# Fewer closing waits on SyncE, and denominators one group later, in a two-branch attention kernel

## The chip, the cores and the metric

One core of one Trainium2 chip. The metric is the device time of one execution in microseconds (us), lower is better. The profile's span is shorter than that time: it runs from the first to the last instruction of the kernel. In the first profiled execution the span was 493.6 us and the time 495.56 us.

All runs of this case were in the fast state, and the mean of TensorE's granted clock over an execution was 0.996 to 1.000 of full speed in all of them.

## The reference, cut to what matters

```python
g = sigmoid((x * gate_w).sum(-1))            # x: 2048 x 1024, bf16
a = A(x)                                     # linear attention, 32 heads of 32
b = B(x)                                     # local attention, 8 keys, every second one
return g * a + (1 - g) * b

# in A: phi(t) = where(t > 0, t + 1, exp(t)) + 1e-6
kv  = einsum("bhsd,bhse->bhde", phi(k), v)
z   = einsum("bhsd->bhd", phi(k))
num = einsum("bhqd,bhde->bhqe", phi(q), kv)
den = einsum("bhqd,bhd->bhq", phi(q), z)[..., None] + 1e-6
o   = num / den                              # then @ wo
```

## The kernel before

The program is written as a list of operations with what they read and write; a small scheduler in Python puts them into an order for each engine, and `emit` adds semaphores. Each DMA channel has a semaphore of its own; there are 81. The scheduler's guess of a DMA's latency decides only the order:

```python
            o.end = t + o.cost
            free[e] = o.end
            fin = o.end
            if o.chan is not None:
                dma_free = max(dma_free, o.end) + o.lat
                fin = dma_free + 2.0          # when users of this DMA may be placed
```

In branch A, queries are taken in four chunks `u` of 512 positions, eight column groups `j` each. When a chunk's eight groups of phi(q) are there, `over(u)` makes the denominators of all heads in one small set of matmuls, inverts them as exp(-ln), sends them to memory and loads them back spread over the partitions, and DVE multiplies phi(q) by them:

```python
        def over(u):
            ...
            P.op("pe", fn, 0.55, mode="c", reads=[zsel.all(), tgt.part((0, 8), (c0, c0 + 512))], ..., name="den")
            R, rs = RAr.next()
            P.op("act", ... ACT.Ln ...); P.op("act", ... ACT.Exp, scale=-1.0 ...)
            for c in range(4):                # store: rc_hbm <- ra
                P.op("sp", ...)
            for j in range(8):                # load: rb <- rc_hbm, then multiply
                B, bs = RBr.next()
                ...
                last_in[0] = P.op("sp", lambda e, B=B, src=src: e.dma_start(B[:, :], src), 0.5, ..., chan="rci%d" % bs, lat=1.0)
                P.op("dve", lambda e, B=B, dst=dst: e.tensor_tensor(dst, dst, B[:, :], ALU.mult), 0.65, reads=[reg, B.all()], writes=[reg])
        ...
        for n, (u, j) in enumerate(nums):
            numer(u, j)
            if j == 7:
                after(3, lambda u=u: over(u))
            slot(0)
```

The formulas used for speed hold only for inputs in a certain range, so the kernel computes a flag, and every engine tests it at its end. If it is 0, a general version (`general_path`) runs and overwrites the output. With this data the flag is 1, so every engine takes a branch over its copy of the general version:

```python
    def tail(e, eng):
        reg = e.alloc_register("fast_ok")
        e.wait_ge(*flag_op.val)
        e.reg_load(reg, flag[0:1, 0:1])
        if eng == "sp":
            for s, v in P.final:              # all 81 DMA channels
                e.wait_ge(s, v)
        with e.If_eq(reg, 0):
            for s, v in P.final + [(P.esem[x], n) for x, n in P.counts.items() if n]:
                e.wait_ge(s, v)
            for th in progs[eng]:             # the general version
                th(e)
```

Of the kernel before, what the change touches and what calls it, by code (L numbers as in the profile page):

```python
# [24 lines left out]
class Tile:  # L25
# [13 lines left out]
    def all(self):  # L39
        return [(self.space, self.lo, self.lo + self.row * self.size, self)]  # L40
# [15 lines left out]


class Op:
    __slots__ = ("eng", "fn", "cost", "deps", "prio", "seq", "chan", "lat", "pos", "val", "users", "raw", "name", "mode", "start", "end")


class Prog:
# [13 lines left out]
        self.held = {}  # L76
        self.read = set()

    def op(self, eng, fn, cost, reads=(), writes=(), prio=None, chan=None, lat=0.0, after=(), name="", mode="m"):
        o = Op()  # L80
        o.eng, o.fn, o.cost, o.prio, o.chan, o.lat, o.name, o.mode = eng, fn, cost, prio, chan, lat, name, mode
        if prio is None:
            o.prio = 1000 + len(self.ops)
        o.seq = len(self.ops)
        o.deps = set(after)
        o.raw = set(after)
        o.users = []
        rd = [iv for r in reads for iv in r]
        wr = [iv for w in writes for iv in w]
        for sp, lo, hi, own in rd:  # L90
            for rec in self.recs.get(sp, ()):
                if rec[0] < hi and lo < rec[1]:
                    if rec[3]:
                        o.deps.add(rec[2])
                        o.raw.add(rec[2])
                    elif sp == "P" and (rec[2].eng != eng or eng == "any"):
                        o.deps.add(rec[2])
        for sp, lo, hi, own in wr:
            for rec in self.recs.get(sp, ()):
                if rec[0] < hi and lo < rec[1]:  # L100
                    o.deps.add(rec[2])
                    if sp != "P" and rec[4] is not own:
                        o.raw.add(rec[2])
        o.deps.discard(o)
        o.raw.discard(o)
        for sp, lo, hi, own in wr:
            lst = self.recs.setdefault(sp, [])
            lst[:] = [r for r in lst if not (lo <= r[0] and r[1] <= hi)]
            lst.append((lo, hi, o, True, own))
        for sp, lo, hi, own in rd:  # L110
            self.recs.setdefault(sp, []).append((lo, hi, o, False, own))
        for sp, lo, hi, own in rd + wr:
            if sp == "P" and own is not None:
                self.held.setdefault(own, []).append(o)
                if eng != "pe":
                    self.read.add(own)
        self.ops.append(o)
        return o

    def schedule(self, dma_rate=0.2e6):  # L120
        for o in self.ops:
            for d in o.deps:
                d.users.append(o)
        left = {o: len(o.deps) for o in self.ops}
        ready_at = {o: 0.0 for o in self.ops}
        free = {e: 0.0 for e in self.ENGS}
        dma_free = 0.0
        wait = {e: [] for e in self.ENGS}
        avail = {e: [] for e in self.ENGS}

        def ready(o, at):
            if o.eng == "any":

                est = []
                for e in ("act", "dve"):
                    q = sum(x[2].cost for x in avail[e] if x[0] < o.prio) + sum(x[2].cost for x in wait[e] if x[2].prio < o.prio and x[0] < at + 0.3)
                    est.append((max(free[e], at) + q + o.cost[e], e))
                o.eng = min(est)[1]
                o.fn, o.cost = o.fn[o.eng], o.cost[o.eng]
            heapq.heappush(wait[o.eng], (at, o.seq, o))  # L140

        for o in self.ops:
            if left[o] == 0:
                ready(o, 0.0)
        self.order = {e: [] for e in self.ENGS}
        mode = "m"
        done = 0
        while done < len(self.ops):
            best = None
            for e in self.ENGS:  # L150
                while wait[e] and wait[e][0][0] <= free[e]:
                    _, _, o = heapq.heappop(wait[e])
                    heapq.heappush(avail[e], (o.prio, o.seq, o))
                if avail[e]:
                    t = free[e]
                elif wait[e]:
                    t = wait[e][0][0]
                else:
                    continue
                if best is None or t < best[0]:  # L160
                    best = (t, e)
            assert best is not None, "no operation can go"
            t, e = best
            if not avail[e]:
                while wait[e] and wait[e][0][0] <= t:
                    _, _, o = heapq.heappop(wait[e])
                    heapq.heappush(avail[e], (o.prio, o.seq, o))
            _, _, o = heapq.heappop(avail[e])
            if e == "pe":

                if o.mode != mode and mode != "m":
                    near = [x for x in avail[e] if x[2].mode == mode and x[0] < o.prio + 30]
                    if near:
                        x = min(near)
                        avail[e].remove(x)
                        heapq.heapify(avail[e])
                        heapq.heappush(avail[e], (o.prio, o.seq, o))
                        o = x[2]
                if o.mode != mode:
                    t += 0.09  # L180
                mode = o.mode
            o.start = t
            o.end = t + o.cost
            free[e] = o.end
            fin = o.end
            if o.chan is not None:
                dma_free = max(dma_free, o.end) + o.lat
                fin = dma_free + 2.0
            o.pos = len(self.order[e])
            self.order[e].append(o)  # L190
            done += 1
            for u in o.users:
                lat = self.LAT[o.eng] if (u.eng != o.eng or o in u.raw) and o.chan is None else 0.0
                if u.eng == o.eng == "pe":
                    lat = 0.0
                ready_at[u] = max(ready_at[u], fin + lat)
                left[u] -= 1
                if left[u] == 0:
                    ready(u, ready_at[u])
        self.span = max(free.values())  # L200

    def emit(self, block, tail):
        for e in self.ENGS:
            self.esem[e] = self.sem("e_" + e)
        chan_n = {}
# [5 lines left out]
        for o in order:  # L211
# [10 lines left out]
            deps = sorted(o.deps, key=lambda d: -d.start)  # L222
            for d in deps:
# [3 lines left out]
                s, v = d.val  # L227
# [16 lines left out]
            tail(e, eng)  # L244

        self.final = [(self.csem[c], n) for c, n in chan_n.items()]
        self.counts = cnt
        block.sync(lambda e: run(e, "sp"))
        block.scalar(lambda e: run(e, "act"))
# [853 lines left out]
def build_kernel(nc, A_x, A_wqkv, A_wo, B_x, B_wqkv, B_wo, gate_w, out):  # L1103
# [117 lines left out]
    def plan(seen):  # L1221
# [241 lines left out]
        def after(n, f, cols=False):  # L1463
            later.append((slot_n[0] + n, f, cols))
            later.sort(key=lambda x: x[0])
# [112 lines left out]
        def over(u):  # L1578
# [16 lines left out]
            for j in range(8):  # L1595
                B, bs = RBr.next()
                src = rc_hbm[u, 4 * j:4 * j + 4, :, :].rearrange("r k n -> (r k) n")[:, None, :].to_broadcast([16, 8, 512])
                last_in[0] = P.op("sp", lambda e, B=B, src=src: e.dma_start(B[:, :], src), 0.5, reads=[[("R", 4 * u + j // 2, 4 * u + j // 2 + 1, None)]], writes=[B.all()],  # L1598
                                  chan="rci%d" % bs, lat=1.0)
                dst, reg = tgt[:, j, c0:c0 + 512], tgt.part((j, j + 1), (c0, c0 + 512))  # L1600
                P.op("dve", lambda e, B=B, dst=dst: e.tensor_tensor(dst, dst, B[:, :], ALU.mult), 0.65, reads=[reg, B.all()], writes=[reg])  # L1601

# [46 lines left out]
        for n, (u, j) in enumerate(nums):  # L1649
            numer(u, j)  # L1650
            if j == 7:
                after(3, lambda u=u: over(u))
            slot(0)
            if n in (2, 4, 6, 8):
                fold((n - 2) // 4, (n - 2) // 2 % 2)
            if n >= 20:
                a_out(*outs.pop(0))
                slot(0)
# [48 lines left out]
    def tail(e, eng):  # L1707
        reg = e.alloc_register("fast_ok")
        e.wait_ge(*flag_op.val)
        e.reg_load(reg, flag[0:1, 0:1])  # L1710
        if eng == "sp":
            for s, v in P.final:
                e.wait_ge(s, v)
        with e.If_eq(reg, 0):
            for s, v in P.final + [(P.esem[x], n) for x, n in P.counts.items() if n]:
                e.wait_ge(s, v)
            for th in progs[eng]:
                th(e)
# [37 lines left out]
```

## Time and profile before

| | |
|---|---|
| time, median of the first 3 runs | 495.04 us (494.76 to 495.15) |
| span of the profiled execution | 493.6 us |
| TensorE busy | 97% of the span, granted clock 0.998 |
| longest TensorE wait after 320 us | 0.98 us, third denominator |
| last store issued / landed | 488.97 / 491.05 us |
| SyncE's 81 waits | 490.00 to 492.82 us |

The page of the kernel before: the span; the busy time, share and instruction count of each engine; and the chain that ended last.

```profile
span 493.6 us, 11394 instructions
PE 477.7 (97%) x5055; PEld 226.2 (46%) x5121; DVE 274.7 (56%) x487; ACT 166.9 (34%) x287; POOL 5.1 (1%) x27
...
PE 89%; DMA 3%; SPq 3%; issue 2%; DVE 2%; ACT 1%; ACTq 0%
```

TensorE bounds this kernel. (5055 matmuls against 5121 weight loads: 66 matmul records are missing from this trace, so the busy time is a little too low.) What is to be won lies in TensorE's few waits, in the head before it starts, and in the tail after it ends. The table of TensorE's waits from 320 to 494 us names one wait worth a look: engine, line, what it waited for, total us, times, longest us.

```profile
PE ps_all L1585 <- DVE xT L1326: 1.0, 1, 1.0
PE ps_all L1313 <- issue: 0.3, 2, 0.2
```

The timeline around it (start, duration, engine, line, operation, count, and in brackets the idle time ahead with what ended it) shows how it comes about. L1601 is the multiplication by the reciprocals, L1326 the last step of phi, L1585 the denominator matmul.

```profile
362.04 0.69 DVE L1601 TENSOR_TENSOR xT<-xT,rb 128x512 bf16<-128x512 bf16 x1 [1.38 <-DMA rb<-rc_hbm]
...
369.60 0.69 DVE L1601 TENSOR_TENSOR xT<-xT,rb 128x512 bf16<-128x512 bf16 x1 [1.00 <-DMA rb<-rc_hbm]
370.21 0.68 DVE L1326 SCALAR_TENSOR_TENSOR xT<-ps_all,e 128x512 bf16<-128x512 f32 x1
370.95 0.62 PE L1585 MATMUL ps_all<-xT,zsel 128*32 128x512 bf16 x8 [0.98 <-DVE xT L1326]
```

DVE stands 1.38 and 1.00 us at multiplications whose reciprocals have not landed; the phi behind them in its queue starts only at 370.21 us, behind the multiplication of 369.60 us, and TensorE waits 0.98 us for it.

The tail is not on the page, since waits and branches are not counted as busy. It stands in the trace's records of single instructions, printed here (start in us, duration in ns, operation, semaphores that it waits for):

```
Sync   488.971  432 DMA_DIRECT2D      last store
Sync   489.459  503 TENSOR_LOAD       the flag
Sync   490.004   28 EVENT_SEMAPHORE   173, 172
...    38 more with two waits each, about 61 ns apart
Sync   492.790   28 EVENT_SEMAPHORE   212, 133
Sync   492.857   58 COMPARE_BRANCH    132
Sync   493.362   57 DRAIN
Vector 488.655   72 COMPARE_BRANCH
Vector 491.538   58 DRAIN
```

### The profile page before, as it was taken

Reading aid. Unit: us, or ns where it says so; the run is one execution under the profiler, and the core shown is the slowest. Engines: PE = TensorE matmul, PEld = TensorE weight load, DVE = VectorE, ACT = ScalarE, POOL = GpSimd, SP = SyncE. Lnnn points to the kernel's source line nnn. Section 1 sums busy time; section 2 is a strip of 40 time slices with the busy share of each in tenths; the row PEclk is TensorE's granted clock in tenths of the full one; section 3 lists DMA queues with packets and bytes.
Section 4 is the critical chain, followed back from the end, with each engine's and each line's share of the span. In section 5 each row is a group of like instructions: output and inputs, shape, how many; then the busy total and the mean of one; then the engine's idle time right before and its main releaser. Section 6 shows DMA issues by size and latency. Waiting matters only on the chain.

```text
span 493.6 us, 11394 instructions
## 1 busy us (share of the span) xinstructions
PE 477.7 (97%) x5055; PEld 226.2 (46%) x5121; DVE 274.7 (56%) x487; ACT 166.9 (34%) x287; POOL 5.1 (1%) x27
## 2 busy tenths in 40 slices
PE   8999999999999999999999999999999999999995
PEld 3444444444444445545554544444444444444442
DVE  2112345899676785564555555596865735524443
ACT  2111111222334345656565465455432223020000
POOL 3000000000000000000000000000000000000000
PEclk9999999999999999999999999999999999999999
DMA  8989992222003155111010100503564325101122
GB/s 225 212 206 322 307 371 62 86 86 85 14 23 110 29 161 141 28 36 35 24 35 25 35 3 3 171 1 80 124 182 117 76 38 153 65 1 66 65 85 68
DMA packets 51067, 48.80 MB, mean 99 GB/s; under 512 B 20161, under 2 KB 38977, under 8 KB 51010
## 3 DMA queue, kind: packets, MB, share of 16 engines
q1 hardware_dynamic: 50466, 47.47, 34.5%
q8 instruction: 42, 0.69, 0.6%
q10 hardware_dynamic: 544, 0.52, 0.3%
q14 instruction: 15, 0.12, 0.1%
HBM read 34.34 MB, written 9.44 MB: 89 GB/s over the span
## 4 chain that ended last, share of the span: by engine, by line
PE 89%; DMA 3%; SPq 3%; issue 2%; DVE 2%; ACT 1%; ACTq 0%
PE ps_all L1313 71%; PE ps_all L1634 11%; PE ps_all L1405 2%; PE ps_all L1424 2%; DMA rb<-rc_hbm 1%; SPq L1287 1%; PE ps_all L1506 1%; SPq L1598 1%; DMA w<-in_B_wqkv_dram 1%; PE ps_all L1431 1%; DMA rc_hbm<-ra 1%; DVE zsel L1548 1%; SPq L1292 1%; DVE pq L1326 0%; PE ps_all L1585 0%
## 5 line engine op out<-in xcount | busy, mean ns | idle before, releaser
L1313 PE MATMUL ps_all<-w,xT 128*128 128x512 bf16 x921 | 207.5, 380 | 5.4 <-issue 4.3
L1313 PE MATMUL ps_all<-xT,w 128*128 128x512 bf16 x748 | 167.5, 379 | 2.3 <-issue 1.7
L1313 PEld LDWEIGHTS ps_all<-w,xT 128*128 128x128 bf16 x960 | 91.3, 98 | 109.8 <-DMA xT<-in_A_x_dram 1.8
L1313 PEld LDWEIGHTS ps_all<-xT,w 128*128 128x128 bf16 x768 | 73.7, 98 | 89.1 <-issue 1.8
L1634 PE MATMUL ps_all<-w,qT 128*128 128x512 bf16 (+1 forms) x259 | 55.3, 373 | 0.3
L1634 PEld LDWEIGHTS ps_all<-w,qT 128*128 128x128 bf16 x264 | 25.8, 98 | 29.7
L1324 DVE TENSOR_SCALAR e<-e 128x512 bf16<-128x512 bf16 x64 | 18.3, 291 | 33.8 <-ACT e L1320 17.2
L1344 DVE CAST vst<-ps_all 128x512 bf16<-128x512 f32 x15 | 10.4, 692 | 44.0 <-PE ps_all L1313 44.0
L1411 ACT ACTIVATE E<-ps_all 128x1824 bf16<-128x1824 f32 (+1 forms) x18 | 30.4, 1687 | 9.8 <-PE ps_all L1405 9.0
L1322 ACT ACTIVATE e<-ps_all 128x512 bf16<-128x512 f32 x32 | 19.1, 597 | 42.8 <-PE ps_all L1313 42.8
L1414 DVE TENSOR_TENSOR E<-E,msk 128x1824 bf16<-128x1824 bf16 (+1 forms) x18 | 19.8, 1102 | 22.1 <-ACT E L1411 22.1
L1638 DVE SCALAR_TENSOR_TENSOR o<-ps_all,gm,xT 128x512 bf16<-128x512 f32 (+1 forms) x25 | 18.2, 730 | 23.0 <-PE ps_all L1634 22.8
L1320 ACT ACTIVATE e<-ps_all 128x512 bf16<-128x512 f32 x32 | 19.1, 597 | 26.8 <-PE ps_all L1313 25.8
L1345 ACT ACTIVATE vst<-ps_all 128x512 bf16<-128x512 f32 x17 | 10.1, 597 | 47.7 <-PE ps_all L1313 47.7
L1274 DVE TENSOR_TENSOR mx<-mx,kT 128x1024 bf16<-128x1024 bf16 x32 | 20.8, 688 | 9.3 <-ACT kT L1345 9.2
L1274 DVE TENSOR_TENSOR mx<-mx,qT 128x1024 bf16<-128x1024 bf16 x32 | 20.8, 687 | 6.9 <-ACT qT L1348 6.7
L1443 DVE TENSOR_TENSOR qT<-ps_all,L 128x456 bf16<-128x456 f32 (+1 forms) x36 | 21.0, 627 | 6.2 <-ACT L L1441 5.0
L1326 DVE SCALAR_TENSOR_TENSOR pk<-ps_all,e 128x512 bf16<-128x512 f32 x32 | 21.9, 688 | 0.7
L1440 ACT ACTIVATE L<-ps_all 128x456 f32<-128x456 f32 (+1 forms) x36 | 17.8, 547 | 12.4 <-PE ps_all L1424 12.4
L1345 ACT ACTIVATE kT<-ps_all 128x512 bf16<-128x512 f32 x16 | 9.6, 597 | 35.8 <-PE ps_all L1313 35.8
L1601 DVE TENSOR_TENSOR xT<-xT,rb 128x512 bf16<-128x512 bf16 x24 | 16.3, 689 | 8.7 <-DMA rb<-rc_hbm 8.5
L1348 ACT ACTIVATE qT<-ps_all 128x512 bf16<-128x512 f32 x16 | 9.6, 597 | 31.5 <-PE ps_all L1313 31.5
(72 smaller groups left out, 284.1 us busy)
## 6 DMA issues: line engine op xcount, KB each, us to landing
rb<-rc_hbm SPq DMA_DIRECT2D x32, 256.0 KB, 5.1
w<-in_A_wqkv_dram SPq DMA_DIRECT2D x6, 1024.0 KB, 8.5
v<-vB_hbm SPq DMA_DIRECT2D x36, 128.0 KB, 2.9
vB_hbm<-vst SPq DMA_DIRECT2D x32, 128.0 KB, 5.9
w<-in_B_wqkv_dram SPq DMA_DIRECT2D x4, 1024.0 KB, 9.0
xn<-in_A_x_dram SPq DMA_DIRECT2D x16, 256.0 KB, 2.7
out_dram<-o SPq DMA_DIRECT2D x15, 256.0 KB, 2.0
w<-in_A_wo_dram SPq DMA_DIRECT2D x8, 256.0 KB, 4.1
```

What stands on the lines that cost most here:

```text
L1274: P.op("dve", lambda e, m=m, op=op: e.tensor_tensor(m[:, 0:n], m[:, 0:n], src, op), 0.08 + n / 1920.0, reads=[m.all(), reg], writes=[m.all()],
L1313: last = e.matmul(bank.ap(), lhs(dc), rhs(dc), start=(dc == 0), stop=(dc == 7))
L1320: P.op("act", lambda e: e.activation(e_[:, :], bank.ap(), ACT.Exp), act(512), reads=[bank.iv], writes=[e_.all()])
L1322: P.op("act", lambda e: e.activation(e_[:, :], bank.ap(), ACT.Exp, accum_out=qe[:, col:col + 1]), act(512) + 0.1, reads=[bank.iv], writes= ...
L1324: P.op("dve", lambda e: e.tensor_scalar(e_[:, :], e_[:, :], 1.0, 1e-6, op0=ALU.min, op1=ALU.add), 0.25, reads=[e_.all()], writes=[e_.all()])
L1326: P.op("dve", lambda e: e.scalar_tensor_tensor(out=dst, in0=bank.ap(), scalar=0.0, in1=e_[:, :], op0=ALU.max, op1=ALU.add), dps(512), read ...
L1345: fa = lambda e: e.activation(dst, src(), ACT.Copy)
L1411: P.op("act", lambda e: e.activation(E[:, 0:32 * nq].rearrange("p (j q) -> p j q", j=4), ps[:, 4:8, 0:8 * nq], ACT.Exp), act(32 * nq), rea ...
L1414: P.op("dve", lambda e: e.tensor_tensor(ev(), ev(), m[:, :, :].rearrange("p r q -> p (r q)")[:, None, :].to_broadcast([128, 16, 2 * nq]), ...
L1443: P.op("dve", lambda e, L=L, h=h, q0=q0: e.tensor_tensor(qT[:, :, q0:q0 + nq], SO[h].ap(0, n).rearrange("p (c q) -> p c q", c=8), L[:, 0:n ...
L1634: last = e.matmul(bank.ap(0, f1 - f0), qT[:, dc, t * 128:(t + 1) * 128], ws[3][:, dc, f0:f1], start=(dc == 0), stop=(dc == 7))
L1638: P.op("dve", lambda e, bank=bank, o_=o_, t=t, n=n, i0=i0, i1=i1, tgt=tgt, c0=c0: e.scalar_tensor_tensor(out=o_[:, i0 * 128:i1 * 128].rear ...
```

## The change

The intent: SyncE should not go through 81 waits when nearly all of those DMAs have been waited for by somebody who used their data; only the 4 channels of output stores have no other waiter. And the wait on the reciprocals should go away: each chunk's denominators one slot later, and 2.5 us more latency assumed for the loads, so that the scheduler puts the multiplications further back in DVE's queue. The diff, cut to its core:

```diff
-                fin = dma_free + 2.0
+                fin = dma_free + o.pad          # pad=2.0 unless given
...
+    def awaited(self, chan):
+        return all(o.users for o in self.ops if o.chan == chan)
...
         self.final = [(self.csem[c], n) for c, n in chan_n.items()]
+        self.last = [(self.csem[c], n) for c, n in chan_n.items() if not self.awaited(c)]
...
-                                  chan="rci%d" % bs, lat=1.0)
+                                  chan="rci%d" % bs, lat=1.0, pad=4.5)
...
-                after(3, lambda u=u: over(u))
+                after(4, lambda u=u: over(u))
...
         if eng == "sp":
-            for s, v in P.final:
+            for s, v in P.last:
                 e.wait_ge(s, v)
```

More of the change, by code (lines that the diff above doesn't have):

```diff
@@ L58 @@
 class Op:
-    __slots__ = ("eng", "fn", "cost", "deps", "prio", "seq", "chan", "lat", "pos", "val", "users", "raw", "name", "mode", "start", "end")
+    __slots__ = ("eng", "fn", "cost", "deps", "prio", "seq", "chan", "lat", "pos", "val", "users", "raw", "name", "mode", "pad", "start", "end")
 class Prog:
@@ L77, in __init__, with op @@
         self.read = set()
-    def op(self, eng, fn, cost, reads=(), writes=(), prio=None, chan=None, lat=0.0, after=(), name="", mode="m"):
+    def op(self, eng, fn, cost, reads=(), writes=(), prio=None, chan=None, lat=0.0, after=(), name="", mode="m", pad=2.0):
         o = Op()
+        o.pad = pad
         o.eng, o.fn, o.cost, o.prio, o.chan, o.lat, o.name, o.mode = eng, fn, cost, prio, chan, lat, name, mode
```

## The prediction

> **What bounds it.** TensorE. The page gives PE 477.7 of 493.6 us busy (97%), clock 0.998; the chain of waits is 89% PE. From 320 us on, the table of waits has one PE stall of note: the third denominator matmul waits 0.98 us (at 370.95 us) for DVE's phi (L1326), because DVE, in order, stood 1.38 and 1.00 us waiting for reciprocal loads (rb, 362.04 and 369.60 us). The tail: the last matmul ends at 488.0 us, DVE at 488.55, the span at 493.64.
>
> **The tail before, from the instruction records.** SyncE issues the last store at 488.97 us, reads the flag, and goes through 81 waits, two to an instruction: 490.00 to 492.82 us, about 61 ns each. The last store had landed at 491.05 us, so 1.8 us of this is overhead. Then branch 492.86, drain 493.36, and 0.28 us of closing barrier.
>
> **What changes.** Instruction order is identical up to about 334 us.
> 1. The denominators come one to three groups later, and the multiplications that wait for rb stand later in DVE's queue. PE does the same work, so the most to be had is the 0.98 us stall. Normalised chunks stay in time: chunk 0 was multiplied out by 353.1 us, and the first output group that reads it moves later too. I expect -1.0 us.
> 2. 36 SyncE instructions disappear, so SyncE reaches its branch right after the last landing: 1.8 us earlier. But the branch jumps over 145 fallback instructions. [...]branch to drain took 2.88 us on DVE, 2.45 on ACT, 2.54 on POOL, each with an 8 KiB instruction packet about 1 us after the branch[...]. On SyncE it took only 0.50 us. SyncE's own fetches, at 97.0 and 491.6 us, and a 0.4 us hiccup at 490.55 put a block boundary just after its 207th instruction[...]. After the change the branch is about the 203rd instruction, before that boundary[...]. So I estimate that the branch now misses: 2.45 to 2.9 us in place of 0.50, giving back 2.0 to 2.4 us for the 1.8 us saved. Net tail: about +0.4 us. If the fetch was started anyway, the tail gains 1.7 us.
>
> **Sum.** Miss (70%): 495.04 - 1.0 + 0.4 = about 494.4 us. Hit (30%): 495.04 - 1.0 - 1.7 = about 492.3 us. Median 494.2 us; 8 in 10: 492.0 to 495.0. Faster by over 2%: 0.01; within 2%: 0.98; slower: 0.01.
>
> **What would show it.** (a) The wait of the denominator matmul on DVE's phi goes from 0.98 us to about 0, and the last matmul ends about 1 us earlier. (b) SyncE has 2 wait instructions before the branch, and the branch starts within 0.15 us of the last landing. (c) Branch to drain on SyncE grows to about 2.5 us, with a new 8 KiB instruction fetch after the branch; if (c) is absent, the hit case.
>
> **What would make it wrong.** A straggling last landing (one of 16 came 0.38 us after the others); a new PE wait on a normalised chunk; the fetch being ahead of where I place it.

(In this text instructions are counted from 0: the branch is number 239 before and 203 after, its target 385 and 349. Two of the expectations below count the same ones from 1.)

What the trace of before shows: branch to drain took 2.88 us on DVE, 2.45 on ACT and 2.54 on POOL, each with an 8 KiB instruction packet 0.92 to 1.05 us after the branch (489.70, 444.57 and 433.45 us); on SyncE it took 0.50 us, and packets start at 491.58 and 492.36 us, 1.27 and 0.50 us ahead of that branch, the next one at 493.92 us, after the drain. Which of them are SyncE's the author read from their times. That a fetch makes the difference, and that a boundary lies behind number 207, is the estimate from these times and the 0.40 us hiccup; the expectations below call it the fetch theory, and group 2 tests where the branch turns slow.

## The result, and the profile after

495.53 us median (495.31 to 496.11, 6 runs) against 495.1 us (494.76 to 496.3, 6 runs): ratio 1.0008, 95% interval 0.9995 to 1.002. Ratios here are the mean time of one kernel's fast runs over that of the other's of the same rounds, so not quite the ratio of the medians. The forecast was 494.2 us, 492.0 to 495.0: the class (within 2%) was right, the range was missed by 0.5 us.

The table of TensorE's waits after, same stretch, has only its headings: the wait is gone.

```profile
core 0 of [0], span 494.1 us
engine line waited for: us in total, times, longest us
```

The timeline after at the same place (lines of the file have moved by 6: L1607, L1332 and L1591 answer to L1601, L1326 and L1585):

```profile
370.76 0.69 DVE L1607 TENSOR_TENSOR xT<-xT,rb 128x512 bf16<-128x512 bf16 x1 [0.33 <-DMA rb<-rc_hbm]
...
372.12 0.69 DVE L1332 SCALAR_TENSOR_TENSOR xT<-ps_all,e 128x512 bf16<-128x512 f32 x1
372.69 0.61 PE L1591 MATMUL ps_all<-xT,zsel 128*32 128x512 bf16 x8
```

SyncE's tail, by single instructions as above:

```
Sync   489.024  433 DMA_DIRECT2D      last store (landed 491.250)
Sync   489.514  517 TENSOR_LOAD       the flag
Sync   491.084   17 EVENT_SEMAPHORE   211
Sync   491.267   28 EVENT_SEMAPHORE   212, 209
Sync   491.337   58 COMPARE_BRANCH    208
Sync   493.857   63 DRAIN             2.52 us after the branch (before: 0.50)
```

Both parts of the forecast are there: no wait, and a branch that reaches its place 0.09 us after the last landing and then takes 2.52 us. From the end of the last DVE operation to the span's end it is 5.57 us now, 5.09 before. Yet TensorE's last matmul started at 487.77 us, as before (487.76): the microsecond of the wait did not come out. It had been lost at the other end. The timelines of both at the first score matmul (a matmul of branch B), of before:

```profile
5.62 14.69 PE L1313 MATMUL ps_all<-w,xT 128*128 128x512 bf16 x62 [0.35 <-DMA xT<-in_A_x_dram]
...
125.78 0.70 PE L1405 MATMUL ps_all<-qT,kT 32*64 32x57 bf16 x64
```

and of after:

```profile
5.97 14.37 PE L1319 MATMUL ps_all<-w,xT 128*128 128x512 bf16 x58 [0.70 <-DMA xT<-in_A_x_dram]
...
126.89 0.70 PE L1411 MATMUL ps_all<-qT,kT 32*64 32x57 bf16 x64
```

TensorE's instructions up to here stand in the same order in both kernels. The first matmuls that wait for a load start 0.35 us later, and the first score matmul came 1.11 us later (the stretch up to it is called the head from here on). With that the two traced executions add up: 1.11 us longer to the first score matmul, 1.10 us shorter from there to the last matmul, 0.31 us longer after it, together 0.32 us, which is the difference of their times (495.88 and 495.56 us). So the first question for the chip was whether this is chance of one execution or belongs to the changed program; the second, whether the slow branch is what the prediction takes it for; the third came from the answers.

### The profile page after: what moved, and what is told of

It is laid out like the page before. It is cut to its first block, busy times and chain, and to the rows that moved or that the text cites. A ratio compares the mean times of both kernels' runs of the same rounds, so it can differ in the third digit from the quotient of the medians.

```text
span 494.1 us, 11425 instructions
## 1 busy us (share of the span) xinstructions
PE 486.0 (98%) x5121; PEld 226.8 (46%) x5121; DVE 273.7 (55%) x486; ACT 167.7 (34%) x288; POOL 5.1 (1%) x27
## 4 chain that ended last, share of the span: by engine, by line
PE 96%; DVE 2%; DMA 1%; issue 0%
PE ps_all L1319 78%; PE ps_all L1640 11%; PE ps_all L1411 2%; PE ps_all L1430 2%; DMA xT<-in_A_x_dram 1%; PE ps_all L1512 1%; PE ps_all L1437 1%; DVE zsel L1554 1%; PE ps_all L1591 0%; DVE pq L1332 0%; PE ps_all L1564 0%; DVE e L1330 0%; DVE w L1350 0%; DVE o L1644 0%; DVE kvT L1550 0%
## 5 line engine op out<-in xcount | busy, mean ns | idle before, releaser
L1319 PE MATMUL ps_all<-w,xT 128*128 128x512 bf16 x960 | 215.1, 381 | 0.7 <-DMA xT<-in_A_x_dram 0.7
L1319 PE MATMUL ps_all<-xT,w 128*128 128x512 bf16 x768 | 170.5, 379 | 0.0
L1326 ACT ACTIVATE e<-ps_all 128x512 bf16<-128x512 f32 x32 | 19.1, 597 | 26.8 <-PE ps_all L1319 25.7
L1332 DVE SCALAR_TENSOR_TENSOR pk<-ps_all,e 128x512 bf16<-128x512 f32 x32 | 21.9, 687 | 0.7
L1354 ACT ACTIVATE xT<-ps_all,g 128x512 bf16<-128x512 f32 x14 | 9.3, 686 | 35.6 <-PE ps_all L1319 35.6
```

Of the source, the lines that this page charges most:

```text
L1319: last = e.matmul(bank.ap(), lhs(dc), rhs(dc), start=(dc == 0), stop=(dc == 7))
L1326: P.op("act", lambda e: e.activation(e_[:, :], bank.ap(), ACT.Exp), act(512), reads=[bank.iv], writes=[e_.all()])
L1332: P.op("dve", lambda e: e.scalar_tensor_tensor(out=dst, in0=bank.ap(), scalar=0.0, in1=e_[:, :], op0=ALU.max, op1=ALU.add), dps(512), read ...
L1354: fa = lambda e: e.activation(dst, src(), ACT.Copy, scale=scale)
```

## The experiments

Fifteen runs, in four groups; the kernels of a group ran on one chip beside 11 runs of the kernel before. All were correct.

### Group 1: the same again, and each half alone

`before_again` and `after_again` are unchanged. `waits_only` and `den_only` are the changed kernel with one half undone:

```diff
# waits_only
-                                  chan="rci%d" % bs, lat=1.0, pad=4.5)
+                                  chan="rci%d" % bs, lat=1.0)
-                after(4, lambda u=u: over(u))
+                after(3, lambda u=u: over(u))
# den_only
-            for s, v in P.last:
+            for s, v in P.final:
```

> The kernel before, unchanged. In the first pair of traces the first score matmul started at 125.78 us before and at 126.89 us after, although both kernels have the same instructions up to there. If this is chance of one execution, it moves here by some tenths of a us to 1 us from 125.78; if it belongs to the program, it stays within 0.2 us of 125.78. The stall before the third denominator is about 1 us again (0.5 to 1.4), SyncE's branch to drain 0.5 us, ratio 1.000 within 0.002.

> The changed kernel, unchanged. Chance: the first score matmul is nearer to 126 us and the time about 0.6 us below the kernel before (0.9988). Program: 126.9 us again and about 0.4 us above (1.0008). Either way SyncE's branch to drain 2.5 us and no denominator stall.

> The short closing waits alone, denominators as before. Fetch theory (the branch is the 202nd SyncE instruction, its target the 348th[...]): branch to drain 2.5 us, the stretch from the last DVE operation's end to the span's end about 5.5 us in place of 5.09, time +0.4 us against before (1.0008), with the 1 us stall still there. Rival (the waits themselves cost): the stretch falls to about 3.3 us, time -1.8 us (0.9965).

> The later denominators and the longer assumed latency alone, all 81 closing waits kept (branch the 242nd instruction, target the 388th[...]). Stall theory: no denominator stall, last stretch about 5.1 us, branch to drain 0.5 us, time -1.0 us against before (0.998), if the head of the kernel lasts as long as before. Rival (the change of order makes the head longer by the program): the first score matmul at 126.9 us, time as before (1.000).

| run | ratio to before, 95% interval | first score matmul | from it to last matmul | branch to drain, SyncE |
|---|---|---|---|---|
| before_again | 0.9993 (0.9981 to 1.0006) | 125.58 | 362.00 | 0.51 |
| after_again | 0.9988 (0.9975 to 1.0001) | 127.20 | 360.92 | 2.73 |
| waits_only | 1.0012 (1.0000 to 1.0024) | 126.37 | 361.62 | 2.72 |
| den_only | 0.9975 (0.9962 to 0.9988) | 125.89 | 360.92 | 0.51 |

By the ratios, the later denominators alone gain 0.25% (1.2 us); the short waits alone lose 0.12% (0.6 us), with an interval that begins at 1.0000. Their product, 0.9987, is what the changed kernel showed on this chip, and also what the prediction's larger case said (494.4 over 495.04 is 0.9987). The table of TensorE's waits of waits_only still has the wait, shorter in this execution; that of den_only does not.

```profile
PE ps_all L1591 <- DVE xT L1332: 0.6, 1, 0.6
```

### Group 2: moving the branch by a few instructions

In before, SyncE's closing waits start 0.06 to 0.09 us apart, but behind number 207 the next one starts 0.40 us later (490.55 to 490.95 us). If the branch is slow ahead of this place and short behind it, a few more instructions ahead of the branch must bring the 0.5 us back as soon as they push it past number 207. `pad4` and `pad8` add 4 and 8 instructions of two long satisfied waits each, before a store for which SyncE stands idle anyway (17 waits for DVE at the output stores in before, 65.4 us in all):

```diff
+        PAD, PER = 4, 4                      # 8, 8 in pad8
+        early_x = [(self.csem["x%d" % i], 16) for i in range(16)]
         def run(e, eng):
...
+                if left and i > stop:        # once, ahead of the fourth last store
+                    m = min(PER, left); left -= m
+                    for q in range(2 * m):
+                        e.wait_ge(*early_x[q % 16])
```

`branch_first` lets the far branch run beside the landing of the last store, by waiting after it; `pad20_branch_first` does both:

```diff
-        if eng == "sp":
-            for s, v in P.last:
-                e.wait_ge(s, v)
         with e.If_eq(reg, 0):
             ...
+        if eng == "sp":
+            for s, v in P.last:
+                e.wait_ge(s, v)
```

> The changed kernel with 4 more SyncE instructions (each two waits that were satisfied long ago), put where SyncE idles between output stores. Its branch becomes instruction 207, counted from 0, the last one before the block boundary that I place between 207 and 208; its target is 353. Fetch theory: still a miss, branch to drain 2.5 to 2.75 us with an 8 KiB instruction packet about 1 us after the branch, time equal to the changed kernel within noise. Rival (the branch is slow because SyncE had been standing at a wait for the last landing): 2.5 us as well.

> The same with 8 instructions: branch 211, target 357, the boundary is crossed about 1.8 us before the branch. Fetch theory: [...]branch to drain about 0.5 us, the span ends about 2.0 us earlier measured from the end of the last DVE operation (3.5 in place of 5.6 us), time 1.6 to 2.2 us below the changed kernel (about 0.996 against before). Rival (standing at the wait makes the branch slow): 2.5 us, no gain.

> The changed kernel with the four closing waits after the branch instead of ahead of it; nothing padded (branch 201[...]). Fetch theory: the branch still costs 2.5 us, but from about 490.0 us on, beside the landing of the last store, so the span ends about 4.3 us after the last DVE operation (5.6 in the changed kernel), 1.3 us less time than the changed kernel. Rival (standing at the wait makes the branch slow): the branch, now ahead of the waits, takes 0.5 us, and the end is at about 3.3 us after the last DVE operation, 2.2 us less.

> Both: 20 padding instructions and the waits after the branch. Branch to the first wait 0.5 us, SyncE ready at the last landing (about 2.6 us after the last DVE operation). The end is then set by DVE's own branch, 2.9 us to its drain, so about 3.3 us after the last DVE operation, 2.2 us below the changed kernel (about 0.995 of before). Rival (closing waits and branch are not what ends the kernel): no gain over pad8 or the changed kernel.

| run | branch, target | branch to next instruction | span's end past the last DVE operation | median time, ratio |
|---|---|---|---|---|
| pad4 | 207, 353 | 2.78 | 5.86 | 494.86, 0.9983 (0.9966 to 1.0001) |
| pad8 | 211, 357 | 0.69 | 3.84 | 494.35, 0.9975 (0.9957 to 0.9992) |
| branch_first | 201, 347 | 2.72 | 4.85 | 494.49, 0.9975 (0.9958 to 0.9993) |
| pad20_branch_first | 221, 367 | 0.52 | 3.40 | 494.32, 0.9972 (0.9955 to 0.9988) |

(The third and fourth columns, in us, are read from the traces that were kept of these runs. In at least three of the four the kept trace is of another execution than the timed one, by its span, so its own measured time is not known.)

The fetch theory agrees with this. Four instructions between pad4 and pad8 take 2.09 us off the branch (2.78 and 0.69 us), though both stand at the same wait for the same landing; so the rival is out. In pad4's records two instruction packets of 8 KiB start at 491.05 and 491.21 us, 0.8 and 1.0 us after the branch, and none of that size in the 1.6 us ahead of it; in pad8's one starts at 489.65 us, 1.01 us before the branch. branch_first is slow (2.72 us) although it does not stand at a wait. The branch is slow as number 207 and short as number 211, on the sides that the hiccup in the trace of before gave them. What a packet holds, and so whether the branch waits for one, no trace shows.

But the times do not follow the spans. The median span of pad8's runs is 1.7 us shorter than that of pad4's, and pad20_branch_first's 0.5 us shorter still, and the median times differ by only 0.51 and 0.03 us. So two expected gains were missed: pad8 was to gain 1.6 to 2.2 us and branch_first 1.3 us on the changed kernel, and against pad4, which is that kernel but for four instructions, they gained 0.51 and 0.37. Over all runs the time was 1.7 to 1.8 us longer than the span in pad4, 1.8 to 2.3 in branch_first, 2.9 to 3.1 in pad8, and 3.3 to 3.5 in pad20_branch_first. Something else ends the execution.

### Group 3: what ends the measured time

In the kept traces of before, after and group 1 the time was 4.0 to 4.7 us past the start of DVE's drain (its last instruction but one, after the branch); with those of group 2 the author put the least at 3.7 us. DVE, too, takes a far branch (over 792 instructions, 2.9 us), right after its last operation. If DVE's end is the other limit, then delaying only DVE's branch must lengthen the time without lengthening the span, and taking it away from the end must shorten both.

`dve_spread` is the kernel before with 128 satisfied-wait instructions on DVE, 8 ahead of each of its last 16 operations, where DVE idles (0.97 or 0.98 us ahead of most of them in before); `dve_late` puts the last 16 of them behind its last operation instead:

```diff
+        SPREAD, LATE = 14, 16                # 16, 0 in dve_spread
...
+                if eng == "dve" and i >= len(plan[eng]) - SPREAD:
+                    for q in range(16):
+                        e.wait_ge(*early_x[q])
...
+            if eng == "dve":
+                for q in range(2 * LATE):
+                    e.wait_ge(*early_x[q % 16])
             tail(e, eng)
```

`early_branch` is the changed kernel with the flag test of SyncE and DVE moved ahead of their last 6 and 10 operations. These stand in the program twice, once in the fallback and once behind it, so the fallback still computes what it did (with this data it never runs; no run here tries it):

```diff
+        REST = {"sp": 6, "dve": 10}
...
+            n = len(plan[eng]) - REST.get(eng, 0)
+            ops(plan[eng][:n])
+            tail(e, eng, lambda: ops(plan[eng][n:]))
...
         with e.If_eq(reg, 0):
+            rest()
             ...                              # waits, general version
+        if eng in ("sp", "dve"):
+            with e.If_ne(reg, 0):
+                rest()
+        if eng == "sp":
+            for s, v in P.last:
+                e.wait_ge(s, v)
```

> The changed kernel with the flag test of SyncE and DVE moved ahead of their last 6 and 10 operations (which then stand twice in the program, once in the fallback and once after it), so that both take their far branch, 2.5 to 2.9 us, between two output tiles, some 12 us before the end; four closing waits at the very end. In the eight traces so far the measured time is 6.75 to 7.7 us past the end of the last DVE operation, wherever the span ends (1.7 to 3.5 us of it past the span's end), and 3.7 us past DVE's drain at the least. Theory DVE (DVE's far branch and what is fetched after it set the end of the measured time): the branch gone from the end, time 1.5 to 2.5 us below pad8 and the later denominators alone, about 0.993 of before. Rival (something else that follows a fixed time after the last matmul or the last store, such as TensorE's own branch): span ends near 490.8 us, time as pad8, 0.9975.

> Control for the next: the kernel before with 128 more DVE instructions (two long satisfied waits each), 8 ahead of each of its last 16 operations, where DVE idles about 1 us for each tile.[...] Both theories: last DVE operation within 0.3 us of before, time as before (0.999 to 1.001).

> The same 128 instructions, but the last 16 of them stand after the last DVE operation, ahead of DVE's flag test: DVE's branch comes about 1 us later (489.6 for 488.66), still 0.8 us ahead of SyncE's last wait, so that the span should end as in the control, at 5.1 us past the last DVE operation. Theory DVE: the measured time grows by 0.7 to 1.0 us against the control all the same (1.0015 to 1.002). Rival (SyncE's 81 waits end the measured time of the kernel before): no change, 1.000.

> The later denominators alone once more, beside the others on this chip: 0.9975 of before again, no denominator stall, and the first score matmul within 0.3 us of 125.9 us if its head is not long by chance.

| run | median time, ratio | time minus span, all runs |
|---|---|---|
| early_branch | 491.78, 0.9919 (0.9902 to 0.9936) | 1.7 to 1.8 |
| dve_spread | 496.06, 1.0005 (0.9988 to 1.0022) | 1.8 to 2.0 |
| dve_late | 496.92, 1.0016 (1.0001 to 1.0030) | 3.1 to 3.6 |
| den_only_2 | 494.43, 0.9966 (0.9953 to 0.9980) | 1.7 to 2.1 |

dve_late took 0.86 us more than its control by the medians, while the median of its six spans was the shorter one (493.6 against 494.2 us). The intervals of the two ratios overlap, so the verdict rests on the last column: in every run of dve_late the time lies over 3 us past the span, in every run of the control 2 us or less. (TensorE's wait at the denominators, 1.5 us in dve_late's trace and 0.4 in the control's, does not touch that column, since it lengthens span and time alike. One miss: in the traced execution of dve_late, DVE's drain came 4.75 us past its last operation, 1.35 us more than in the control where about 1.0 was expected, and so the span's end fell together with it.)

early_branch removes it from the end. Its timeline shows DVE's branch as a longer pause between two tiles, in the brackets of the second line, and DVE in step again five tiles on (the pause of 1.78 us between comes without a wait that the trace names):

```profile
471.07 0.75 DVE L1649 SCALAR_TENSOR_TENSOR o<-ps_all,gm,xT 128x512 bf16<-128x512 f32 x1 [0.97 <-PE ps_all L1645]
474.77 0.75 DVE L1649 SCALAR_TENSOR_TENSOR o<-ps_all,gm,xT 128x512 bf16<-128x512 f32 x1 [2.94 <-PE ps_all L1645]
477.31 2.07 DVE L1649 SCALAR_TENSOR_TENSOR o<-ps_all,gm,xT 128x512 bf16<-128x512 f32 x3 [1.78 <-issue]
479.71 0.75 DVE L1649 SCALAR_TENSOR_TENSOR o<-ps_all,gm,xT 128x512 bf16<-128x512 f32 x1 [0.34 <-PE ps_all L1645]
...
484.89 1.36 DVE L1649 SCALAR_TENSOR_TENSOR o<-ps_all,gm,xT 128x512 bf16<-128x512 f32 x2 [0.97 <-PE ps_all L1645]
```

TensorE does not wait for it: its matmuls run on in one stretch of 16.80 us from 469.80 us. The far branch took 2.97 us on DVE and 2.76 us on SyncE, as at the end, and costs nothing there; the second test, whose branch is not taken, took 0.09 to 0.10 us. Ratio 0.9919: about 4 us below the kernel before, and 2.7 us below den_only_2 on the same chip (difference of the medians; 1.5 to 2.5 were expected). It beats both kernels. The edit moves both engines' branches; that DVE's is the one that counts follows from group 2, where taking SyncE's out of the way brought next to nothing. TensorE's own branch, which the expectation names as a rival, stayed where it was.

One line describes the thirteen kept traces whose own time was measured (all but the four of group 2): the time is the later of (span's end + 1.74 us) and (DVE's drain + 3.75 us), both counted from the start of the span. The two constants are fitted, no more, and what the measured time begins with no trace shows.

| traced execution | span's end + 1.74 | DVE's drain + 3.75 | measured |
|---|---|---|---|
| before | 495.38 | 495.29 | 495.56 |
| after_again | 496.40 | 495.61 | 496.40 |
| pad8_2 (group 4) | 493.42 | 494.47 | 494.33 |
| dve_late | 496.29 | 498.02 | 498.04 |
| early_branch | 491.45 | 490.40 | 491.44 |

The largest miss of the thirteen is 0.31 us (before_again). In the kernel before the two limits lie within 0.1 us of each other: by this line SyncE's 81 waits ended just when DVE's own end would have ended the execution. What takes 3.75 us past DVE's drain no trace here shows, since the kernel's instructions are over; only instruction packets are seen, the last of them 0.6 to 0.8 us before the measured end in every one of the thirteen but early_branch's (1.9 us). That part stays open.

### Group 4: is the longer head the program's?

`after_third` is the changed kernel, `pad8_2` is pad8 again, and `after_dead36` puts 36 instructions into SyncE's fallback, so that the program is as long as before:

```diff
             for s, v in P.final + [(P.esem[x], n) for x, n in P.counts.items() if n]:
                 e.wait_ge(s, v)
+            if eng == "sp":
+                for q in range(72):
+                    e.wait_ge(*P.final[q])
```

> The changed kernel once more, on another chip perhaps. So far 1.0008 and 0.9988 of before; its two traced executions had the first score matmul at 126.89 and 127.20 us, 1.0 to 1.5 us later than most others. Chance theory (the head varies from execution to execution in any kernel): ratio about 0.999 (stall -1.0 us, tail +0.5 us), spans of most runs about 0.5 us below before's. Program theory (a shorter SyncE program makes the head longer): ratio 1.000 to 1.001, first score matmul past 126.5 us again.

> The changed kernel with 36 SyncE instructions put back into the fallback block, which is never run: the program is as long as before, the branch still far from its target (203 to 385, a miss). Chance theory: as the changed kernel on this chip. Program theory: the head is as in before (125.6 us) and the time 0.7 to 1.0 us below the changed kernel.

> The kernel whose SyncE branch finds its target fetched, beside the changed kernel on one chip. If the measured time is the later of (span's end + 1.74 us) and (DVE's drain + 3.75 us), which fits all 14 traces within 0.35 us: the span ends 1.8 to 2.0 us earlier than in the changed kernel, but the time falls by only 0.5 us, since DVE's end then holds.

| run | median time, ratio | first score matmul | from it to last matmul |
|---|---|---|---|
| after_third | 494.92, 0.9989 (0.9976 to 1.0002) | 125.83 | 360.87 |
| after_dead36 | 495.14, 1.0001 (0.9984 to 1.0017) | 126.01 | 360.87 |
| pad8_2 | 494.31, 0.9981 (0.9964 to 0.9998) | 126.03 | 360.88 |

The unchanged changed kernel now has its first score matmul at 125.83 us, where two earlier executions had 126.89 and 127.20. That one was on another chip; but on the chip of after_again too the traced execution was the odd one, with a span of 494.7 us against 493.1 to 493.4 us in the same kernel's other four. The timeline of after_third, for comparison with the two above:

```profile
6.04 2.07 PE L1319 MATMUL ps_all<-w,xT 128*128 128x512 bf16 x8 [1.35 <-DMA xT<-in_A_x_dram]
8.31 12.04 PE L1319 MATMUL ps_all<-w,xT 128*128 128x512 bf16 x55 [0.20 <-DMA xT<-in_A_x_dram]
...
125.83 0.70 PE L1411 MATMUL ps_all<-qT,kT 32*64 32x57 bf16 x64
```

So the head of one kernel differs by up to 1.4 us between traced executions, and the length of the program has no visible part in it: after_dead36 is not faster. Over all seventeen traces the head lies between 125.45 and 127.41 us (branch_first), and the first matmul that waits for a load started between 5.6 and 6.1 us.

The traces' record of the granted clock shows the full clock from 6.62 us on in before, but only from 9.43 us in after, 9.91 in after_again and 10.30 in branch_first, the three longest heads (126.89, 127.20, 127.41); in the other fourteen, from 3.96 to 7.14 us, with heads of at most 126.37. The timeline of TensorE from 5.5 to 9.3 us of before,

```profile
5.62 3.87 PE L1313 MATMUL ps_all<-w,xT 128*128 128x512 bf16 x14 [0.35 <-DMA xT<-in_A_x_dram]
```

and of after:

```profile
5.97 3.57 PE L1319 MATMUL ps_all<-w,xT 128*128 128x512 bf16 x8 [0.70 <-DMA xT<-in_A_x_dram]
```

In after each of these eight matmuls starts 0.38 to 0.43 us after the one before it; behind the full clock, and in before from 6.75 us on where no load is awaited, it is 0.22 us. The ninth starts at 8.02 us in before, where it waits for a load, and at 9.34 us in after. By the 41st weight load (14.97 and 16.08 us) the difference is 1.11 us, and it stays so up to the first score matmul. So in the execution behind the result the microsecond was lost to the first loads (0.35 us later) and above all to a clock that came to full speed 2.8 us later; before lost a part of its lead again at a wait of its own at 14.3 us. Why the full clock comes late in some executions no run here shows.

And pad8_2 is 0.61 us below the changed kernel on this chip, close to the 0.5 us expected from the two limits, though its traced span ended 2.0 us earlier (491.68 against 493.74 us).

## Why the prediction was right or wrong

**TensorE bounds the kernel, and the stall is worth 1.0 us: right.** From the first score matmul to the last matmul the two traces of the kernel before took 361.97 and 362.00 us, and the eleven traces with later denominators and no other change to DVE's work took 360.87 to 360.92 us, so 1.1 us. Alone it gave 0.9975 and 0.9966. (The wait itself is no constant: 0.4 to 1.5 us in the five traces with the old order, so that one trace gave its size partly by luck.)

**SyncE's branch now misses, about 2.5 us for 0.5: right in its size.** 2.52 to 2.85 us from branch to drain in all three traces of the changed kernel, 0.5 us in before; the place was put right to within four instructions (number 207 in pad4: 2.78 us; number 211 in pad8: 0.69 us). The packets agree with a fetch as the cause: in the first trace of the changed kernel two of 8 KiB start at 492.14 and 492.28 us, 0.80 and 0.94 us after the branch, and in before two start 1.27 and 0.50 us ahead of it. That it is the cause stays the estimate, since no trace shows what a packet holds.

**Net tail +0.4 us: about right.** From the start of the last matmul to the measured end, the two traces of before took 7.80 and 8.01 us, den_only's two 7.73 and 7.75; the three of the changed kernel 8.11, 8.28 and 8.78. By the means (8.39 against 7.91) that is 0.5 us, with 1.0 us at the most. The last store's landing is now waited for in the open, and it came 2.15 to 2.57 us after its issue in these three (1.67 to 2.60 us over all seventeen traces), which is the straggling landing that the prediction names as a risk.

**The sum and its range: wrong.** The step "495.04 - 1.0 + 0.4 = about 494.4 us", with a range that ended at 495.0, took everything outside the changed parts as fixed: the kernel before's three runs (494.76 to 495.15) as its spread, and its one traced head as every execution's head. In the groups above the kernel before had medians of 495.22 to 495.91 us and single runs from 494.65 to 497.32 us. The term that was sized at zero is the head, which varies by over 1 us, more than the whole effect forecast. In the traced execution behind the result it was 1.11 us longer than in that of before, just what the stall gave, mostly because TensorE had its full clock only from 9.43 us on, against 6.62. For the other five runs of that result there is no trace. Their spans were 493.5 to 494.4 us, against 492.9 to 493.7 in after_third; whether longer heads or later last landings made them so stays open. Later comparisons of the same two kernels gave 0.9988 and 0.9989, where the forecast's larger case was 0.9987: for the program the sum fits (its two terms were each off by 0.1 us, in opposite directions, which is luck); what it left out is how far one comparison of six runs can lie from that. The net effect of the change is a gain of some 0.1% at best, and no single comparison here clears 1.000 with its interval.

**The hit case, 492.3 us: wrong in its size.** It was given 30%, and it did not happen; but it would have been wrong as well. It assumed that the time follows the span. When the branch was made to hit (pad8), the time came to 494.3 us, 0.9975 and 0.9981: no better than the later denominators alone with all 81 waits kept. DVE's own far branch held the end (its drain + 3.75 us gives 494.47 us for pad8_2, the span's end + 1.74 us only 493.42). So hardly any of SyncE's "1.8 us of overhead" was on the path of the measured time: by the two limits, which miss by up to 0.31 us themselves, 0 to 0.24 us of it in the four traces that keep the 81 waits and DVE's end as it was.

## What to carry to other kernels

Before you take instructions away from the end of an engine's queue, ask which other engine ends within a microsecond of it, and where the far branches stand: here removing 36 cheap instructions (0.06 us each) moved a branch from number 239 to number 203 of its queue, and turned 0.50 us into 2.52 (as number 211 it took 0.69 us, as number 207 2.78). If a rarely taken fallback must be jumped over, test for it some operations before the end, where the engine idles; here that was worth more than both parts of the change (0.9919 of before; the later denominators alone 0.9975 and 0.9966). And a forecast of a few tenths of a per cent needs the spread of the untouched parts of the kernel, measured in several executions, before it can have a range.
